# Gate and up projections by seven block products in place of eight, with attention for all tokens moved ahead of the feed-forward part

## The chip, the cores and the metric

The kernel runs on one core of a Trainium2 chip. The metric is device time in microseconds (us). A run that was over 1.5% above the fastest of its kernel counts as slow and is kept out of the ratios.

The engines are named as the profile names them: PE is TensorE (matmuls), PEld its weight loads, DVE is VectorE, ACT is ScalarE, POOL is GpSimd, SP issues the DMAs. In this kernel each engine has its own queue, which keeps the program's order, and waits for the others by semaphores; e1_norm_late below shows what that order alone is worth.

## The reference

A transformer block: pre-norm linear attention with a residual, then a pre-norm gated feed-forward part with a residual. S = 2048 tokens, D = 1024, F = 3584, 32 heads of 32, bf16 inputs.

```python
def _A_ref(x, wqkv, wo):                     # linear attention
    q, k, v = split_heads(x @ wqkv)
    phi = lambda t: where(t > 0, t + 1, exp(t)) + 1e-6
    kv = einsum("bhsd,bhse->bhde", phi(k), v)
    z  = einsum("bhsd->bhd", phi(k))
    o  = einsum("bhqd,bhde->bhqe", phi(q), kv) / (einsum("bhqd,bhd->bhq", phi(q), z)[..., None] + 1e-6)
    return merge_heads(o) @ wo

def _B_ref(x, W_gate, W_up, W_down):         # gated feed-forward
    gate = x @ W_gate
    up   = x @ W_up
    return (gate * (gate > 0) * up) @ W_down

h  = x + _A_ref(layernorm(x), A_wqkv, A_wo)
h2 = h + _B_ref(layernorm(h), B_W_gate, B_W_up, B_W_down)
```

## The kernel before

The kernel is planned in Python: every operation is added to the queue of one engine, and the plan derives the semaphore waits from the buffers that it reads and writes. Each queue keeps the order in which operations were added, so the order of calls is the schedule. Four steps make up the second half of attention:

- `a1(r, ct)`: query projection of one block of 512 tokens and 128 columns (8 matmuls), then the feature map: an exponential on ScalarE and two VectorE steps;
- `a2(st)`: numerators and denominators of a tile of 128 tokens (8 small matmuls), then the division on VectorE;
- `a3`: transpose of the result by DMA;
- `a4(st)`: output projection (16 matmuls), residual, second layer norm.

```python
        def phi(b, w, dst_ap, dst_buf, name):
            ...
            PL.add("act", ... activation(out=Et[:, k, 0:w], in_=src, func=ACTF.Exp) ...)
            PL.add("dve", ... tensor_scalar(E2t, Et, 1.0, 1e-6, op0=ALU.min, op1=ALU.add) ...)
            PL.add("dve", ... scalar_tensor_tensor(dst_ap, src, C1, E2t, op0=ALU.add, op1=ALU.max) ...)

        def a4(r, j, pool):
            ...                                        # 2 x 8 matmuls, residual into hsb
            layernorm(hsb[:, hs, j, :], B_h[hs][j], xn[:, st % NXN, :], B_xn[st % NXN], "dve", "ln2_%d" % st)

        def g_unit(r, ft, pair):                       # one F tile of gate and up, 512 tokens
            for dc in range(NDC):
                mm(bank(ga, SBW), gring[:, sg, dc, fl * P:(fl + 1) * P], hnT[r % 2][:, dc, :], ...)
            for dc in range(NDC):
                mm(bank(gb, SBW), gring[:, su, dc, fl * P:(fl + 1) * P], hnT[r % 2][:, dc, :], ...)
            PL.add("act", ... Relu of bank ga ...)
            PL.add("dve", ... product with bank gb into hhT ...)
```

The feed-forward part handles 512 tokens at a time. The attention steps of the *next* 512 tokens are slipped between its units, so that the numerators and output projections of three of the four token blocks have long runs of gate and up matmuls around them (all query projections come before):

```python
        for r in range(NSB):
            ...
            for ft in range(NFT):
                g_unit(r, ft, pair_of[pidx])
                if bgq:
                    k_, rn, j = bgq.pop(0)
                    run_piece(k_, rn, j, BG)           # one piece of attention of block r + 1
            ...
            for dh in range(ND2):
                d_round(r, dh, ...)                    # down projection
```

## Time and profile before

| | before |
|---|---|
| time, median of 2 | 832.07 us |
| span of the profiled execution | 830.0 us |
| TensorE busy | 99% |
| gate and up matmuls | 1792 |
| spacing of back-to-back 128x512 matmuls | 0.216 us |
| mean granted clock | 1.000 |

The page of the kernel before: busy times, the granted clock in 40 slices (tenths), and the chain of waits followed back from the last instruction.

```profile
PE 823.7 (99%) x4015; PEld 381.3 (46%) x4015; DVE 284.3 (34%) x605; ACT 129.7 (16%) x218; POOL 19.3 (2%) x45
...
PEclk9999999999999999999999999999999999999999
...
PE 98%; DMA 1%; SPq 0%; ACT 0%; DVE 0%; issue 0%; DVEq 0%
```

TensorE is without a wait from 17.6 us on, for 809.4 us, so what counts is the number of matmuls. A busy TensorE is not yet the bound of anything, since records of pipelined matmuls overlap: each lasts 0.38 us in the records, and they start 0.216 us apart. The groups (line, engine, operation, tiles, shapes, count, then busy us and mean ns, then idle time before them) say how many there are. The first two are gate and up, the third is down:

```profile
L474 PE MATMUL ps<-RE,gring 128*128 128x512 bf16 x896 | 196.3, 379 | 0.0
L474 PE MATMUL ps<-RC,gring 128*128 128x512 bf16 x896 | 195.0, 379 | 0.0
L474 PE MATMUL ps<-wdring,RA 128*128 128x512 bf16 x896 | 194.0, 379 | 0.0
```

The timeline of TensorE (start, duration, what) shows attention under cover: numerators (kvz) and output projections (wo) stand between gate and up matmuls (gring), with no idle time in brackets in this stretch:

```profile
203.06 0.63 PE L474 MATMUL ps<-kvz,RB 128*128 128x132 bf16 x8
203.52 3.61 PE L474 MATMUL ps<-RE,gring 128*128 128x512 bf16 x16
...
225.64 3.62 PE L474 MATMUL ps<-wo,RE 128*128 128x512 bf16 x16
229.09 3.62 PE L474 MATMUL ps<-RE,gring 128*128 128x512 bf16 x16
232.55 3.62 PE L474 MATMUL ps<-wo,RE 128*128 128x512 bf16 x16
```

From 229.09 to 232.55 is 3.46 us for 16 matmuls, which is the 0.216 us used throughout.

### The profile page before, as it was taken

The page shows a single profiled execution, that of the slowest core. Times are in us where ns is not written, and L with a number is a line of the kernel's source. Part 1 is how long each engine was busy: PE and PEld are TensorE (multiplying, and loading weights), DVE is VectorE, ACT ScalarE, POOL GpSimd, SP SyncE. Part 2 cuts the span into 40 slices and gives each one's busy share as a digit, 9 for nine tenths or more (in the row PEclk, how much of TensorE's full clock was granted, in tenths as well). Part 3 has the DMA queues.
Part 4 walks back from the last instruction along what each step waited for, and adds up shares of the span by engine and source line. Part 5 has one row for each costly group of instructions (what it writes and reads, how often), then busy time and mean ns, then how long its engine had stood idle before and what let it go on. Part 6 is the DMA issues. An engine that isn't in the chain of part 4 may idle for free.

```text
span 830.0 us, 9935 instructions
## 1 busy us (share of the span) xinstructions
PE 823.7 (99%) x4015; PEld 381.3 (46%) x4015; DVE 284.3 (34%) x605; ACT 129.7 (16%) x218; POOL 19.3 (2%) x45
## 2 busy tenths in 40 slices
PE   8999999999999999999999999999999999999998
PEld 3444444544444444444444444544444444444443
DVE  7455526885552110144511100644111111111111
ACT  4333333312101110001011100111110001111000
POOL 2000000000000000000000000000000000000000
PEclk9999999999999999999999999999999999999999
DMA  9669400230564536545663555555446554443152
GB/s 302 180 188 288 120 13 1 51 78 25 152 177 128 200 104 223 179 131 140 177 187 130 174 182 177 125 173 151 162 150 201 171 159 131 154 151 102 50 167 89
DMA packets 152062, 121.24 MB, mean 146 GB/s; under 512 B 49488, under 2 KB 148048, under 8 KB 152016
## 3 DMA queue, kind: packets, MB, share of 16 engines
q1 hardware_dynamic: 152016, 120.60, 48.3%
q8 instruction: 32, 0.52, 0.3%
q14 instruction: 14, 0.11, 0.0%
HBM read 104.86 MB, written 4.19 MB: 131 GB/s over the span
## 4 chain that ended last, share of the span: by engine, by line
PE 98%; DMA 1%; SPq 0%; ACT 0%; DVE 0%; issue 0%; DVEq 0%
PE ps L474 98%; DMA RB<-in_A_wqkv_dram 1%; SPq L390 0%; PE ps L484 0%; DVE RC L779 0%; ACT Et L533 0%; ACT RA L572 0%; DVEq L112 0%
## 5 line engine op out<-in xcount | busy, mean ns | idle before, releaser
L474 PE MATMUL ps<-RE,gring 128*128 128x512 bf16 x896 | 196.3, 379 | 0.0
L474 PE MATMUL ps<-RC,gring 128*128 128x512 bf16 x896 | 195.0, 379 | 0.0
L474 PE MATMUL ps<-wdring,RA 128*128 128x512 bf16 x896 | 194.0, 379 | 0.0
L754 DVE TENSOR_TENSOR RA<-RC,ps 128x512 bf16<-128x512 bf16 x112 | 76.9, 687 | 249.2 <-PE ps L474 249.2
L752 ACT ACTIVATE RC<-ps 128x512 bf16<-128x512 f32 x112 | 66.9, 597 | 510.3 <-PE ps L474 473.7
L474 PEld LDWEIGHTS ps<-wdring,RA 128*128 128x128 bf16 x896 | 87.7, 98 | 105.7
L474 PEld LDWEIGHTS ps<-RC,gring 128*128 128x128 bf16 x896 | 87.5, 98 | 104.8
L474 PEld LDWEIGHTS ps<-RE,gring 128*128 128x128 bf16 x896 | 87.3, 98 | 103.8
L474 PE MATMUL ps<-RB,RA 128*128 128x512 bf16 x512 | 113.6, 379 | 1.1 <-ACT RA L572 0.7
L779 DVE TENSOR_TENSOR RC<-ps,RF 128x512 bf16<-128x512 f32 x32 | 20.2, 684 | 176.9 <-PE ps L474 176.9
L474 PEld LDWEIGHTS ps<-RB,RA 128*128 128x128 bf16 x512 | 49.1, 98 | 58.3 <-ACT RA L572 0.9
L474 PE MATMUL ps<-wo,RE 128*128 128x512 bf16 x256 | 57.9, 379 | 0.0
L474 PE MATMUL ps<-RA,RC 128*128 128x512 bf16 x256 | 56.7, 379 | 0.0
L533 ACT ACTIVATE Et<-ps 128x512 bf16<-128x512 f32 x64 | 38.2, 597 | 95.5 <-PE ps L474 57.8
L535 DVE TENSOR_SCALAR E2t<-Et 128x512 bf16<-128x512 bf16 x64 | 18.6, 290 | 64.0 <-ACT Et L533 64.0
L474 PEld LDWEIGHTS ps<-wo,RE 128*128 128x128 bf16 x256 | 25.0, 98 | 30.2
L474 PEld LDWEIGHTS ps<-RA,RC 128*128 128x128 bf16 x256 | 24.8, 98 | 29.0
L717 DVE TENSOR_TENSOR RF<-ps,x 128x512 bf16<-128x512 f32 x32 | 22.1, 691 | 24.6 <-PE ps L474 24.5
L512 POOL TENSOR_TENSOR rstd<-ve,neghalf 128x1 f32<-128x1 f32 x32 | 17.5, 548 | 554.5 <-DVE ve L509 554.5
L606 ACT ACTIVATE RE<-ps 128x512 bf16<-128x512 f32 x32 | 19.1, 597 | 36.5 <-PE ps L474 36.5
L538 DVE SCALAR_TENSOR_TENSOR RE<-ps,E2t 128x512 bf16<-128x512 f32 x32 | 22.1, 692 | 1.1
L538 DVE SCALAR_TENSOR_TENSOR RB<-ps,E2t 128x512 bf16<-128x512 f32 x32 | 22.1, 692 | 1.1
(42 smaller groups left out, 168.0 us busy)
## 6 DMA issues: line engine op xcount, KB each, us to landing
gring<-in_B_W_gate_dram SPq DMA_DIRECT2D x28, 1024.0 KB, 5.3
gring<-in_B_W_up_dram SPq DMA_DIRECT2D x28, 1024.0 KB, 7.3
wdring<-in_B_W_down_dram SPq DMA_DIRECT2D x56, 512.0 KB, 3.5
RB<-in_A_wqkv_dram SPq DMA_DIRECT2D x8, 512.0 KB, 8.5
x<-in_A_x_dram SPq DMA_DIRECT2D x16, 256.0 KB, 2.6
out_dram<-RC SPq DMA_DIRECT2D x32, 128.0 KB, 3.8
RE<-in_A_x_dram SPq DMA_DIRECT2D x15, 256.0 KB, 4.7
RC<-in_A_wqkv_dram SPq DMA_DIRECT2D x2, 1024.0 KB, 7.9
```

The costliest lines, as they stand in the source:

```text
L474: lambda e: e.matmul(out_ap, lhsT, rhs, start=start, stop=stop, skip_group_check=skip),
L512: PL.add("pool", lambda e: e.tensor_tensor(out=rstd[:, k, :], in0=ve[:, k, :], in1=neghalf[:], op=ALU.pow), reads=[B_ve[k], B_neghalf], wr ...
L533: PL.add("act", lambda e: e.activation(out=Et[:, k, 0:w], in_=src, func=ACTF.Exp), reads=[B_bank[b]], writes=[B_E[k]], name=name + "_exp")
L535: PL.add("dve", lambda e: e.tensor_scalar(out=E2t[:, k, 0:w], in0=Et[:, k, 0:w], scalar1=1.0, scalar2=1e-6, op0=ALU.min, op1=ALU.add), rea ...
L538: PL.add("dve", lambda e: e.scalar_tensor_tensor(out=dst_ap, in0=src, scalar=C1, in1=E2t[:, k, 0:w], op0=ALU.add, op1=ALU.max), reads=[B_b ...
L606: PL.add("act", lambda e, b=b, j=j: e.activation(out=vv[:, slot, j * GPN:(j + 1) * GPN, 0:P], in_=bank(b, NW).rearrange("p (g w) -> p g w" ...
L717: PL.add("dve", lambda e, b=b, nt=nt: e.tensor_tensor(out=hsb[:, hs, j, nt * NW:(nt + 1) * NW], in0=bank(b, NW), in1=x2[:, xs, nt * NW:(nt ...
L752: PL.add("act", lambda e: e.activation(out=rg[:, k, :], in_=bank(ga, SBW), func=ACTF.Relu), reads=[B_bank[ga]], writes=[B_rg[k]], name="rg ...
L754: PL.add("dve", lambda e: e.tensor_tensor(out=hhT[:, ft, :], in0=rg[:, k, :], in1=bank(gb, SBW), op=ALU.mult), reads=[B_rg[k], B_bank[gb]] ...
L779: PL.add("dve", lambda e, j=j, k=k: e.tensor_tensor(out=outst[:, k, :], in0=bank(banks4[j], NW), in1=hsb[:, hs, j, dh * NW:(dh + 1) * NW], ...
```

## The change

The intent is fewer matmuls. Strassen's scheme multiplies 2x2 blocks with 7 block products in place of 8. Here the blocks are two token blocks of 512, two halves of D and two F tiles of 128, and gate and up each get 7 products of 4 matmuls per pair of F tiles: 56 matmuls, where the plain way takes 64. The price is sums: four sums `S` of activations per pass, four sums `T` of weights for each weight block (fp16, on VectorE), copies of partial results in PSUM (ScalarE), and more elementwise work at the end.

A pass needs both token blocks at once and room for them, so the feed-forward part now runs in two passes of 1024 tokens, and attention for *all* 2048 tokens comes first. The residual and the normalized tokens of the second pass go to scratch space in DRAM and come back. The normalization of the second layer norm moved from VectorE to ScalarE, with a helper step on GpSimd.

The diff, cut to its core:

```diff
+        def a4(st):
+            ...                                             # 16 matmuls into two banks
+            PL.add("dve", ... tensor_tensor(out=hsb[:, hs, :], in0=ps[:, b:b + 2, :], in1=x2, op=ALU.add) ...)
+            ...
+            ks = ln_stats(hsb[:, hs, :], [B_hs[hs]] * NBC, "ln2_%d" % st)
+            PL.add("pool", ... nmr = -mean * rstd ...)
+            PL.add("act", lambda e: e.activation(out=xn[:, kx, :], in_=hsb[:, hs, :], func=ACTF.Identity,
+                                                 bias=nmr[:, ks, :], scale=rstd[:, ks, :]), ...)
+            if st < TPP: dma_t(... hnT ...)                  # first pass: transpose at once
+            else:        dma(... hn_scr ...)                 # second pass: to scratch
...
+            for w in range(2):                               # w: gate, up
+                prod(w, BA[w], w_blk(w, 0, 0), a_blk(0, 0), True, "P1")
+                ident_act(bank(BB[w]), bank(BA[w]), ..., "fk1")
+            for w in range(2):
+                prod(w, BF_[w], t_blk(w, 2), s_blk(2), True, "P7")
+                ident_act(ftmp[:, w, :], bank(BF_[w]), ..., "s7")
+            for w in range(2):
+                prod(w, BB[w], t_blk(w, 1), s_blk(1), False, "P6")
+                ident_act(bank(BC_[w]), bank(BB[w]), ..., "fk2")
+            ...                                              # P2, P5, P4, P3 in the same way
...
+        rest = [(r, ct) for r in range(1, NSB) for ct in range(NG)]
+        LAG = 2
+        for t in range(NST):
+            a2(t)
             if rest:
+                a1(*rest.pop(0))
+            if t >= LAG:
+                a4(t - LAG)
+            if rest:
+                a1(*rest.pop(0))
+            if t == 13:
+                s_sums()
+            if t == 14:
+                for f_ in t_sums(0) + t_sums(1):
+                    f_()
...
+        for p_ in range(NPASS):
+            for q in range(NPAIR):
+                ...
+                strassen_pair(p_, q, fill)
+            for i, (hf, dh) in enumerate(rounds):
+                if p_ + 1 < NPASS and i == 0:
+                    for t in range(TPP):
+                        dma_t(sl_ht[t], hnT[:, :, t * P:(t + 1) * P], hn_scr[t * P:(t + 1) * P, :], ...)
+                d_round(p_, hf, dh, [0, 1, 2, 3] if i % 2 == 0 else [4, 5, 6, 7])
```

## The prediction

> **What bounds it now.** TensorE. The chain of waits is 98% matmuls: one unbroken run of 809.4 us (3936 records) from 17.6 us; granted clock 1.000. Groups: 1792 gate/up and 896 down matmuls; in the timeline 16 of them start 3.455 us apart in total, 0.216 us each. VectorE is busy 34%, ScalarE 16%. The Trainium skill, "TensorE: Matmul & The Clock Gate", section "Back-to-back issue gap", gives N/2.4+2.5 = 216 ns for N=512; the trace agrees.
>
> **What the change removes.** 7 products for 8: gate/up goes from 1792 to 1568 matmuls, 224 x 0.216 = 48.4 us, all on the critical path. Fp16 operands should run at the same rate. Weight traffic for gate/up halves; DMA is not critical.
>
> **What it adds, feed-forward.** A pair of F tiles is 56 matmuls, 12.1 us (28 pairs). Per pair, ScalarE gets 10 evictions (0.6 us each: 6 us) and VectorE 8 operations of about 0.65 us plus 8 weight sums. The skill's "VectorE: DVE Perf Modes", section "The perf-mode tier table", gives tensor_tensor on 16-bit SBUF data 2x, so I estimate (256+150)/0.96 = 0.42 us for a sum (0.69 if 1x): 8.5 to 10.5 us of 12.1. Each copy that a product accumulates upon has two to three products (1.7 to 2.6 us) of slack. So Strassen should remain TensorE-bound. The eight transposes reread between passes (1.24 us issue each) fit before the fifth down-weight chunk is needed (14 us).
>
> **What it moves.** Attention loses its cover. Before, three quarters of it hides under gate/up matmuls; now a tile's iteration holds only numerators (0.46), two query projections (2 x 1.73) and one output projection (3.45): 7.4 us of TensorE. VectorE needs 2.05 (divide) + 2 x 0.92 (feature maps) + about 2.9 (residual and statistics) = 6.8 us, but it doesn't flow: normalization now sits on ScalarE between the two exponentials of an iteration, behind two GpSimd steps. VectorE, in order, waits for the second exponential: statistics end -> rstd (0.80 in the trace) -> negated mean (about 0.4) -> normalization of 1024 (about 1.2) -> exponential (0.6), about 3 us idle. Period about 9.8 us, and TensorE follows through the numerators' single set of banks. Ten such iterations: +24 us. Then:
> - first numerators wait for the last feature map: +2 (another 1 or 2 at token-block boundaries);
> - the last four tiles have no projections left: VectorE-bound (5 against 3.9 us per tile), with the S sums (about 5 us) and first T sums (3.4 us) before the last divisions, and the last output projection waiting for its transpose (about 3.3 us): +15;
> - clock lost after 4 to 6 us gaps: +2.
>
> Lost: about 44 of 48 us. Attention, from the first query projection to the first Strassen product, takes about 160 us instead of 117 us of TensorE work.
>
> **Prediction: 826 us**, 8 in 10 within 805 to 845. Faster by over 2%: 0.24; within 2%: 0.69; slower: 0.07.
>
> **What would show it.** (a) TensorE busy falls to about 775 to 780 us; the Strassen stretches have TensorE idle near 0 and 12.1 us a pair. (b) TensorE idle of some 40 us lies in the attention stretch (about 130 to 290 us), ended by VectorE's division or feature map. (c) VectorE's second feature-map step shows about 3 us wait per tile for the exponential, which waited for the normalization, which waited for GpSimd. (d) Largest single gaps, 4 to 6 us, just before Strassen begins.
>
> **What would make it wrong.** Faster: the GpSimd/ScalarE detour is shorter, or TensorE's lead absorbs it: toward 800. Slower: weight sums at 1x (+6 at the attention's end, less slack per pair), mixed fp16/bf16 matmuls slower, clock throttled in attention's repeated 2 to 3 us gaps, or transposes delaying the first down weights.

## The result, and the profile after

| | before | after |
|---|---|---|
| time, median of 2 | 832.07 us | 852.77 us |
| span of the profiled execution | 830.0 us | 849.7 us |
| TensorE busy | 823.7 us (99%) | 791.0 us (93%) |
| VectorE busy | 284.3 us | 433.2 us |
| mean granted clock | 1.000 | 0.972 |

The ratio of after to before is 1.0248, with a 95% interval of 1.0207 to 1.0288: slower. Ratios here are the mean time of one kernel's fast runs over that of the other's fast runs of the same rounds, so not quite the ratio of the medians. All outputs, here and in every run below, agreed with the reference.

The page after, the same parts:

```profile
PE 791.0 (93%) x3719; PEld 362.6 (43%) x3791; DVE 433.2 (51%) x900; ACT 245.8 (29%) x402; POOL 25.2 (3%) x60
...
PEclk9999999989897899999999989999999999999999
...
PE 81%; DVE 9%; issue 4%; SPq 2%; ACT 1%; POOL 1%; DMA 1%; DVEq 0%; ACTq 0%; POOLq 0%
```

TensorE is no longer alone on the chain, and its clock drops in four of the slices 9 to 14 (170 to 297 us, attention) and in slice 24 (500 us, between the passes). The waits of TensorE (who waited for whom: us in total, times, longest us):

```profile
PE ps L499 <- DVE RAB L538: 24.2, 7, 6.7
...
PE ps L499 <- DVE RO L674: 11.7, 11, 5.6
...
PE ps L499 <- DMA RW<-in_B_W_down_dram: 6.9, 1, 6.9
...
PE ps L499 <- ACT ps L755: 2.8, 1, 2.8
...
PE ps L499 <- DMA RO<-RO: 2.1, 1, 2.1
```

`RAB L538` is the feature map, `RO L674` the division, `RW` a chunk of down weights, `ps L755` a copy of a Strassen partial result, `RO<-RO` the last transpose of attention.

Now one iteration of attention in the timeline, with the chain that paces it (the bracket at the end is the idle time of that engine before it, and what ended it):

```profile
167.63 1.22 DVE L698 TENSOR_TENSOR hsb<-ps,RX 128x1024 bf16<-128x1024 f32 x1
...
170.44 0.15 DVE L514 TENSOR_SCALAR ve<-mv 128x1 f32<-128x1 f32 x1
170.68 0.55 POOL L517 TENSOR_TENSOR rstd<-ve,neghalf 128x1 f32<-128x1 f32 x1 [9.11 <-DVE ve L514]
171.33 0.26 POOL L706 TENSOR_SCALAR nmr<-mv,rstd 128x1 f32<-128x1 f32 x1
171.71 1.24 ACT L710 ACTIVATE xn<-hsb,nmr,rstd 128x1024 bf16<-128x1024 bf16 x1 [7.81 <-POOL nmr L706]
172.85 0.58 ACT L533 ACTIVATE RX<-ps 128x512 bf16<-128x512 f32 x1
173.46 0.29 DVE L535 TENSOR_SCALAR RX<-RX 128x512 bf16<-128x512 bf16 x1 [2.87 <-ACT RX L533]
173.79 0.69 DVE L538 SCALAR_TENSOR_TENSOR RAB<-ps,RX 128x512 bf16<-128x512 f32 x1
...
174.54 0.29 PE L499 MATMUL ps<-kvz,RAB 128*128 128x132 bf16 x1 [6.54 <-DVE RAB L538]
174.62 3.62 PE L499 MATMUL ps<-RAB,RC 128*128 128x512 bf16 x8
178.03 3.74 PE L499 MATMUL ps<-RW,RO 128*128 128x512 bf16 x15
...
182.23 1.23 DVE L698 TENSOR_TENSOR hsb<-ps,RX 128x1024 bf16<-128x1024 f32 x1 [2.25 <-PE ps L499]
```

VectorE ends the statistics (the line `ve`, 170.44 + 0.15) at 170.6 and has nothing to do until 173.46, although the projection whose exponential it waits for was finished long before: ScalarE, in order, first had to do the normalization, which waited for GpSimd. The iteration shown is also one at the end of a token block. There the next numerators need the last feature map, so TensorE, in order, stands still for 6.5 us, and then does the next query projection and output projection, which VectorE in turn waits for. Eight matmuls take about 3.4 us here (174.62 to 178.03), where 1.73 is normal: after the gap TensorE runs at half rate. An iteration inside a block has the same wait of VectorE (2.87 us again, at 188.08 and 198.16).

The residual additions (`hsb`) of tiles 0 to 9 start at 157.54, 167.63, 182.23, 192.33, 202.42, 212.64, 226.63, 236.86, 247.09 and 257.66: a spacing of 10.1 to 10.6, and of about 14 at the two token-block boundaries. The matmuls of an iteration come to 7.37 us.

Between the passes, the queue that issues the DMAs, then TensorE:

```profile
475.75 0.37 SPq L432 DMA_DIRECT2D wring<-in_B_W_up_dram  x1
476.17 12.21 SPq L436 DMA_TRANSPOSE hnT<-hn_scr  x8
488.56 1.87 SPq L432 DMA_DIRECT2D RX<-h_scr  x4
490.53 2.73 SPq L432 DMA_DIRECT2D RW<-in_B_W_down_dram  x4
```

```profile
475.49 13.98 PE L499 MATMUL ps<-RW,RAB 128*128 128x512 bf16 x63
496.39 3.88 PE L499 MATMUL ps<-RW,RAB 128*128 128x512 bf16 x11 [6.93 <-DMA RW<-in_B_W_down_dram]
```

Four chunks of down weights, 14 us of matmuls, are there in advance. The fifth could have been asked for after the first chunk, near 479; it was issued at 490.53, behind eight transposes and four reloads of the residual, and landed 5.8 us later.

And the first Strassen pair (P1 at 301.73, P7 at 303.46, then P6):

```profile
303.46 1.89 PE L499 MATMUL ps<-RC,RE 128*128 128x512 f16 x8
308.12 3.50 PE L499 MATMUL ps<-RC,RE 128*128 128x512 f16 x8 [2.77 <-ACT ps L755]
```

P6 accumulates on a copy that ScalarE makes of P1. That copy stands in ScalarE's queue behind the normalizations of the last tiles.

The account closes. Counts times spacing give 830.0 - 224 x 0.216 = 781.6 us if TensorE had only lost the matmuls. The span is 849.7, so 68.1 us were lost:

| stretch | from, to | takes | its matmuls | lost |
|---|---|---|---|---|
| first query projection to first Strassen product | 128.4, 301.7 | 173.3 | 118.0 | 55.3 |
| first Strassen pair | 301.73, 318.36 | 16.6 | 12.1 | 4.5 |
| first pass's down rounds | 475.49, 580.62 | 105.1 | 96.7 | 8.4 |
| sum (68.1 from the spans; the rest is rounding) | | | | 68.2 |

The other 27 Strassen pairs follow each other at 12.09 us, with no wait.

### The profile page after: what moved, and what is told of

The parts are those of the page before. It is cut to its first block, busy times and chain, and to the rows that moved or that the text cites. A ratio compares the mean times of both kernels' runs of the same rounds, so it can differ in the third digit from the quotient of the medians.

```text
span 849.7 us, 9959 instructions
## 1 busy us (share of the span) xinstructions
PE 791.0 (93%) x3719; PEld 362.6 (43%) x3791; DVE 433.2 (51%) x900; ACT 245.8 (29%) x402; POOL 25.2 (3%) x60
## 4 chain that ended last, share of the span: by engine, by line
PE 81%; DVE 9%; issue 4%; SPq 2%; ACT 1%; POOL 1%; DMA 1%; DVEq 0%; ACTq 0%; POOLq 0%
PE ps L499 81%; DVE st L509 2%; DVE hsb L698 2%; DVE RO L674 1%; SPq L436 1%; ACT RX L533 1%; DVE RAB L538 1%; DVE RX L535 1%; DMA RW<-in_B_W_down_dram 1%; POOL rstd L517 1%; DVE rden L667 0%; DVE RC L728 0%; DVE dtmp L663 0%; DVE mv L512 0%; DMA RO<-RO 0%
## 5 line engine op out<-in xcount | busy, mean ns | idle before, releaser
L499 PE MATMUL ps<-RW,RAB 128*128 128x512 bf16 x878 | 194.3, 381 | 7.9 <-DMA RW<-in_B_W_down_dram 6.9
L499 PE MATMUL ps<-RC,RE 128*128 128x512 f16 x672 | 156.0, 382 | 2.8 <-ACT ps L755 2.8
L499 PEld LDWEIGHTS ps<-RW,RAB 128*128 128x128 bf16 x896 | 87.9, 98 | 113.9 <-DMA RW<-in_B_W_down_dram 7.4
L499 PE MATMUL ps<-RAB 128*128 128x512 bf16 x499 | 112.4, 379 | 1.6 <-ACT RAB L571 0.7
L755 ACT ACTIVATE ps<-ps 128x512 f32<-128x512 f32 x112 | 65.1, 582 | 161.2 <-PE ps L499 160.6
L499 PE MATMUL ps<-hnT,wring 128*128 128x512 bf16 x448 | 105.8, 379 | 0.0
L499 PEld LDWEIGHTS ps<-RC,RE 128*128 128x128 f16 x672 | 66.0, 98 | 83.3 <-ACT ps L755 3.3
L755 ACT ACTIVATE RO<-ps 128x512 f32<-128x512 f32 x112 | 66.7, 597 | 53.9 <-PE ps L499 53.9
L499 PE MATMUL ps<-RW,RO 128*128 128x512 bf16 x249 | 62.4, 403 | 2.7 <-DMA RO<-RO 2.1
L499 PE MATMUL ps<-RAB,RC 128*128 128x512 bf16 x250 | 64.2, 407 | 0.4
L710 ACT ACTIVATE xn<-hsb,nmr,rstd 128x1024 bf16<-128x1024 bf16 x16 | 19.8, 1240 | 114.1 <-POOL nmr L706 114.1
L755 ACT ACTIVATE RAB<-ps 128x512 bf16<-128x512 f32 x56 | 33.4, 597 | 62.0 <-PE ps L499 62.0
L499 PE MATMUL ps<-kvz,RAB 128*128 128x132 bf16 x128 | 14.2, 230 | 36.6 <-DVE RAB L538 24.2
```

Source lines behind the costliest of these rows:

```text
L499: lambda e: e.matmul(out_ap, lhsT, rhs, start=start, stop=stop, skip_group_check=skip),
L710: PL.add("act", lambda e: e.activation(out=xn[:, kx, :], in_=hsb[:, hs, :], func=ACTF.Identity, bias=nmr[:, ks, :], scale=rstd[:, ks, :]), ...
L755: PL.add("act", lambda e: e.activation(out=dst, in_=src, func=func), reads=reads, writes=writes, name=name)
```

## The experiments

Theory A says that queue order did this: the normalization stands between two exponentials, and VectorE, TensorE and the DMA queue each wait in order for something that they need not wait for. Rival B says that VectorE is simply too full once attention has lost its cover (6.8 us of work per 7.4 us). Rival C puts it on the clock.

Times are compared with the changed kernel's 852.77, which was not run again beside them; ratios are against before, run on the same chip. The kernel before took 832.07 us in the changed kernel's rounds and 831.5 and 831.8 in those of the experiments, so the two comparisons differ by under 0.1%.

### e1_norm_late: the normalization after the second projection

```diff
-            ks = ln_stats(...)                      # then nmr, norm2 and its DMA, all in a4
+            ln2_k[st] = ln_stats(...)
+        def a4n(st):                                # nmr, norm2 and its DMA
             ...
                 a4(t - LAG)
             if rest:
                 a1(*rest.pop(0))
+            if t >= LAG:
+                a4n(t - LAG)
```

> The changed kernel with one reorder: the negated mean, the normalization on ScalarE and the transfer behind it are issued after the second query projection of an iteration, not between the two. Nothing else changes, no work is added or removed. Theory A (in-order queues: VectorE waits about 3 us per tile because the second exponential stands behind the normalization on ScalarE): the spacing of the residual additions falls from 10.15 us to 7.4-7.8, at token-block boundaries from 14.2 to about 10; total 815 to 828 us. Rival B (VectorE is simply too full in attention, 6.8 of 7.4 us, so where the normalization stands is irrelevant): within 6 us of the changed kernel's 852. Rival C (the lowered clock is the cause, waits are the effect of nothing in the order): within 6 us too.

Measured: 819.02 us, ratio 0.985 (0.9825 to 0.9876). No operation was added or taken away, and the kernel got 33.7 us faster. The residual additions are now 7.4 us apart inside a block (182.03, 189.28, 196.66) and 9.8 to 11.2 at boundaries. ScalarE does the exponential before the normalization, and VectorE no longer idles:

```profile
183.64 0.60 ACT L533 ACTIVATE RX<-ps 128x512 bf16<-128x512 f32 x1 [2.93 <-PE ps L499]
...
184.85 0.15 DVE L514 TENSOR_SCALAR ve<-mv 128x1 f32<-128x1 f32 x1
184.92 0.28 DVE L535 TENSOR_SCALAR RX<-RX 128x512 bf16<-128x512 bf16 x1
```

VectorE's busy time hardly changed (432.7 against 433.2 us), so rival B falls for this part. The clock rose to 0.987 without anything done to it: it followed the waits, which goes against C as the first cause. (e3 says more on C: it has the old pace at the full clock.)

### e2_norm_twice: the normalization done twice

```diff
-            PL.add("act", ... norm2 ...)
+            for _ in range(2):
+                PL.add("act", ... norm2 ...)
```

> The changed kernel with the normalization on ScalarE done twice (same values written again; the result stays right), which costs ScalarE 16 x 1.15 us while it is idle 71% of the time. Theory A: the normalization lies on the loop that paces attention, so each of about 10 iterations grows by 1.1 us: +8 to +14 us. Rival B (VectorE throughput): 0 to +3 us.

Measured: 868.54 us, 15.8 above the changed kernel, ratio 1.0446. The direction and place are those of A, the size is above the range that I gave. The spacing inside a block grew from about 10.1 to 11.35, and at boundaries from 14.3 to 15.9; from the first to the tenth residual addition that is 12.1 us more. What I had left out is that the doubled step also stands before the first Strassen pair's copies, where TensorE's wait grew from 2.8 to 4.0 us, and before the last tiles. The wait for the down weights, which the edit does not touch, was 8.0 us here against 6.9. An engine that idles 71% of the time passes an extra 1.2 us per tile on in full: 12.1 us over nine intervals are 1.3 each.

### e3_lead_two: two query projections ahead

```diff
         LAG = 2
         fill = []
+        for _ in range(2):
+            a1(*rest.pop(0))
```

> The changed kernel with two query projections of the next token block moved before the first numerators, so that each token block's feature maps are complete one iteration before they are needed. Theory A (at a boundary TensorE, in order, waits for the last feature map and only then starts the projection that VectorE needs next, 4 us per boundary, partly at half clock): three boundaries of 14.2 become 10.15 and the first 1.4 us wait goes: 836 to 842 us. Rival (a boundary only shifts the wait, VectorE's total is what counts): within 4 us of 852.

Measured: 836.12 us, ratio 1.0062 (1.0045 to 1.0079), 16.6 below the changed kernel. The additions are 10.1 to 10.2 us apart up to the ninth (the tenth follows after 9.3), so the boundaries are gone and the pace of the loop is what it was. The clock is 1.00 from 170 to 220 us, the number before the DMA share in this line of stretches (busy us of PE, PEld, DVE, ACT and POOL come first):

```profile
170.00:220.00 50.00, 39.45 (x194) 16.83 (x197) 33.34 (x75) 11.04 (x15) 4.06 (x10) 1.00 0.41 106
```

So rival C falls for the pace inside a block: at the full clock it is still 10.1 us. TensorE waits 1.9 to 2.0 us in each iteration there, and the low clock of the boundaries went with their gaps of 6.5 us. That does not explain all of it: the changed kernel also ran at half rate for some 3 us after waits of 1.6 and 1.8 us inside blocks (from 201.8 and 246.7 on), which similar waits here did not bring. The kernel before also had two query projections issued ahead; the change had dropped them, and e3 puts them back.

### e4_spread: the transposes spread over two down rounds

```diff
-                if p_ + 1 < NPASS and i == 0:
-                    for t in range(TPP):
-                        dma_t(...)                                   # all eight
-                d_round(p_, hf, dh, ...)
+                fl = []
+                if p_ + 1 < NPASS and i < 2:
+                    for t in range(i * TPP // 2, (i + 1) * TPP // 2):
+                        fl.append(lambda t=t: dma_t(...))            # one after each chunk
+                d_round(p_, hf, dh, ..., fill=fl)
```

> The changed kernel with the eight transposes between the passes issued one after each chunk of the first two down rounds, not all before the first. Theory (the 12.2 us of issue on the one queue delay the fifth down-weight chunk, TensorE waits 6.9 us and then runs a while at half clock): the wait goes, 843 to 846 us. Rival (the transposes slow the loads by taking the DMA engines, wherever they stand): the wait is spread, 849 us or more.

Measured: 842.47 us, ratio 1.0133 (1.0117 to 1.0148), 10.3 below the changed kernel and half a microsecond better than the range. In the profiled runs the span fell by 8.3 us, from 849.7 to 841.4. The first pass's down rounds take 96.7 us (475.65 to 572.35), which is their matmuls and nothing else. The fifth chunk is now asked for at 479.35, and TensorE has no gap:

```profile
479.35 0.38 SPq L432 DMA_DIRECT2D RW<-in_B_W_down_dram  x1
479.77 1.55 SPq L436 DMA_TRANSPOSE hnT<-hn_scr  x1
...
475.65 34.70 PE L499 MATMUL ps<-RW,RAB 128*128 128x512 bf16 x157
```

The same loads and transposes go through the same queue, and TensorE does not wait, so it was the order of issue, not the load on the DMA engines.

### e5_plain and e5b_plain: the restructuring without Strassen

```diff
-            ... P1, P7, P6, P2, P5, P4, P3 with their copies ...
+            for n_, (t, h) in enumerate(((0, 0), (0, 1), (1, 0), (1, 1))):
+                for w in range(2):
+                    prod(w, bb[w], w_blk(w, 0, h), a_blk(0, t), True, "M0")
+                    prod(w, bb[w], w_blk(w, 1, h), a_blk(1, t), False, "M1")
+                ident_act(r11[:, n_ % 2, :], bank(bb[0]), ..., "rl", func=ACTF.Relu)
+                PL.add("dve", ... hh = bank(bb[1]) * r11 ...)
-            ... all S and T sums ...
```

> The changed kernel with its order, passes and buffers, but each pair of F tiles computed by the plain 8 block products (64 matmuls) and no S or T sums: the restructuring alone. If Strassen by itself is worth what the count says, this is slower than the changed kernel by 224 x 0.216 = 48.4 us, less about 8 us of sums at the attention's end and up to 4 us of the first pair's wait that plain products do not have: 884 to 896 us, so the restructuring alone costs 52 to 64 us against before. Rival: Strassen's copies and sums cost time in the feed-forward stage itself; then this gains on it there, and the total is under 875.

Measured: 889.73 us (median of four; the three fast ones lie between 888.67 and 889.78), ratio 1.0694 (1.0677 to 1.071). So the new order by itself costs 58 us against before, inside the range, and the rival (under 875) falls. Against the changed kernel it is 37 us slower and not 48.4: there Strassen lost again some 12 us to its own sums before the last divisions (7.6, see below) and to the first pair (4.5). One of its four runs, the one that was profiled, took 1079.26 us at a mean clock of 0.772. It is a slow run, I have no cause for it, and nothing here rests on it. To see the stages, the same kernel was run once more.

> The same kernel as e5_plain again, for a profile in the fast state (the profiled execution of e5_plain had a mean clock of 0.772 and took 1077 us). Feed-forward stretches should show no TensorE waits: a pair takes 64 x 0.216 = 13.8 us against 12.1 with Strassen; the attention's spacing is that of the changed kernel, 10.1 and 14.2 us.

Measured: 888.46 us (one run, so its state is unknown, but it agrees with the fast runs of e5_plain). Its attention has the spacing of the changed kernel (157.82, 167.90, 182.25, ...), and the same 24.2 us of TensorE waits for the feature map. The first product comes at 294.08, 7.6 us earlier than with Strassen, because VectorE has no sums to make before the last divisions.

### e6_three: the three edits together

The edits of e1, e3 and e4.

> The changed kernel with the three edits together: normalization after the second projection, two projections ahead, transposes spread. e1 took 33.7 us, e3 16.6, e4 10.3; e1 and e3 overlap at the token-block boundaries, where e1 still waits some 9 us. Additive otherwise: 796 to 803 us. Left are about 12 us at the end of attention and 4 us in the first pair. If the three are parts of one thing (VectorE's total), the sum stops short: over 808.

Measured: 802.08 us, ratio 0.9641 (0.9627 to 0.9654). Singly the edits took 33.7, 16.6 and 10.3 us, 60.6 in sum; together they took 50.7. That is the range expected, since e1 and e3 both act on the token-block boundaries. TensorE's largest waits are then those at the end of attention and in the first pair:

```profile
245.46 1.45 PE L499 MATMUL ps<-kvz,RAB 128*128 128x132 bf16 x8 [5.56 <-DVE RO L674]
257.64 3.61 PE L499 MATMUL ps<-RW,RO 128*128 128x512 bf16 x15 [2.35 <-DMA RO<-RO]
267.48 3.25 PE L499 MATMUL ps<-RC,RE 128*128 128x512 f16 x8 [2.77 <-ACT ps L760]
```

### e7_five: the first weight sums early, the last normalizations late

```diff
+        t01 = t_sums(0) + t_sums(1)
         for ct in range(NG):
             a1(0, ct)
+            if 3 <= ct <= 6:
+                t01.pop(0)()
+                t01.pop(0)()
...
-            if t == 14:
-                for f_ in t_sums(0) + t_sums(1): f_()
-            a4n(t)                                  # for the last three tiles
+                strassen_pair(p_, q, fill)
+                if p_ == 0 and q < 3:
+                    a4n(13 + q)
```

> e6_three with two more edits: the first eight T sums of weights on VectorE during the first eight query projections, where it is half idle, and the normalizations of the last three tiles (needed in the second pass only) issued after the first, second and third Strassen pair, so that they do not stand before that pair's copies on ScalarE. Expected: 3 us less at the end of attention and 3 to 4.5 us less in the first pair: 789 to 796 us. If the first pair's wait had another cause, over 795.

Measured: 795.4 us, ratio 0.9566 (0.9553 to 0.9579), 6.7 below e6. The total does not decide whether the first pair's wait had the suspected cause (the two ranges, 789 to 796 and over 795, overlap), but the trace does: the wait for ScalarE is gone from the list of waits. Of the two edits made together only the late normalizations touch ScalarE's queue, so they were its cause.

### e8_pool_sums: the first S sums on GpSimd

```diff
-            if t == 13:
-                s_sums()
+            if 10 <= t <= 13:
+                s_sums("pool")[t - 10]()            # one sum per iteration
```

> e7_five with the first four S sums on GpSimd, one per iteration from the eleventh on, not on VectorE after the fourteenth tile. VectorE loses 4.9 us in the stretch where it is the bound: 3 to 5 us less than e7_five. If GpSimd needs over 6 us for a sum of 2048, or the two slow each other, no gain or a loss.

Measured: 790.05 us, ratio 0.9499 (0.9486 to 0.9512), 5.4 below e7, slightly more than expected. A sum takes 4.06 us on GpSimd and 1.22 on VectorE, but GpSimd had the time. TensorE is the chain again, at the full clock. The page's busy times and chain, and what is left of TensorE's waits:

```profile
PE 774.7 (98%) x3719; PEld 359.8 (46%) x3791; DVE 427.5 (54%) x896; ACT 246.9 (31%) x402; POOL 40.5 (5%) x64
...
PE 93%; DVE 4%; issue 1%; ACT 1%; DMA 0%; POOL 0%; SPq 0%; DVEq 0%; ACTq 0%; POOLq 0%
```

```profile
PE ps L499 <- DVE RO L674: 2.6, 7, 0.6
...
PE ps L499 <- DMA RO<-RO: 1.5, 1, 1.5
```

The waits for the feature map, for the down weights and for ScalarE's copies are no longer in the list. Attention takes 125.0 us (128.4 to 253.4) for 118.0 us of matmuls.

### e9_plain_repaired: the repaired order without Strassen

The order of e8 with the plain products of e5, and no sums.

> Attention first with the repairs (normalization late, two projections ahead, transposes spread, last normalizations deferred), but the plain 8 products and no sums. Against e8_pool_sums it lacks only Strassen. If Strassen is worth its 224 matmuls and nothing else: 790 + 48 = 838 us, less up to 2 us of sums that e8 still carries: 835 to 840 us. Then the repaired order alone costs 3 to 8 us against before, and nearly all of the net gain is Strassen's. If Strassen's copies cost anything on TensorE's path: under 832.

Measured: 838.55 us, ratio 1.0085 (1.0071 to 1.0098). Against e8 the difference is 48.5 us, and 224 matmuls at 0.216 us are 48.4. (The two ran on different chips, where the kernel before took 831.5 and 831.8 us.) Strassen pays exactly what it removes, and its sums and copies cost TensorE nothing once they stand in the right place. The repaired order costs 7 us against before.

## Why the prediction was wrong

The prediction was 826 us, within 805 to 845, most likely within 2% of before. Measured were 852.77, slower by 2.5%. The loss of cover and the wait behind the normalization were foreseen, and rightly. The steps that failed are four terms of the sum: the token-block boundaries ("another 1 or 2"), the clock ("+2"), the transposes that "fit", and the slack of the copies in the first pair. Point by point:

1. **What bounded the kernel before, and the gain of 48.4 us.** Right. e9 against e8 shows 48.5. (The formula cited there is the page's for one isolated matmul; see the first point of the last section.)
2. **The feed-forward stretch stays bound by TensorE at 12.1 us a pair.** Right for 27 of 28 pairs (12.09 us), with VectorE's sums at the estimated rate (0.42 us a `T` sum). This agrees with the Trainium skill, "VectorE: DVE Perf Modes", section "The perf-mode tier table", which puts `tensor_tensor` on bf16 data in SBUF at twice the base rate; the trace shows 0.42 us also where bf16 goes in and fp16 comes out. Fp16 and mixed products run at the spacing of bf16: 56 of them in 12.09 us are 0.216 us each.
3. **The loop of attention: "Period about 9.8 us ... Ten such iterations: +24 us".** Right in mechanism and size; VectorE's wait for the exponential, "about 3 us" in the prediction, is 2.87. Inside a token block the spacing is about 10.1; e1 takes the cause away and it falls to 7.4, e2 doubles the suspected step and it rises to 11.35. Over the nine intervals, 10.1 against 7.37 makes 25 us.
4. **Token-block boundaries: "another 1 or 2".** This was the first step that failed: the term was mis-sized. Each of the two boundaries inside the loop took about 4.2 us more than an ordinary interval (14.60 and 13.99 against 10.1), and a third follows after the tenth addition (13.6). I had delayed the numerators by the feature map, but had forgotten that TensorE, in order, holds the next query projection and output projection behind them, which VectorE then waits for: 5.2 us of matmuls, or about 7 where half of the clock is gone. e3, which moves two projections ahead and does nothing else, ends this and gained 16.6 us.
5. **End of attention: "+15" and "clock lost ... +2".** From the tenth addition to the first product 44.1 us passed, and the matmuls that stand behind that tile's output projection come to 24.3 us (some 2 us of them had run before the addition): 19.8 lost. In e3, where the third boundary is gone, the same stretch (250.02 to 285.77) takes 35.8 us for 22.6 us of matmuls, 13.2 lost. So the end alone cost less than the 17 predicted, and the third boundary brought it above. The clock term failed. The prediction expected TensorE idle for "some 40 us" in attention and busy for 775 to 780 us in all. Idle it was for 39.7 us there (173.30 less 133.61 in the first line below, which has the form of the one under e3), but busy for 791.0 in all. The same matmuls kept it busy for 119.67 us in e8 (second line) and for about 14 us more here, at a mean clock of 0.89:

```profile
128.40:301.70 173.30, 133.61 (x630) 60.05 (x641) 118.37 (x271) 34.54 (x46) 13.17 (x29) 0.89 0.34 86
...
128.40:253.40 125.00, 119.67 (x632) 57.24 (x644) 112.83 (x267) 34.34 (x45) 27.84 (x32) 1.00 0.47 121
```

   That the idle time came out as predicted is partly luck, since slow matmuls filled some of the waits. e7 and e8 together got about 12 us out of this stretch and the first pair.
6. **"The eight transposes reread between passes ... fit before the fifth down-weight chunk is needed."** Wrong, and this was another step that failed: 8.4 us. The prediction set 8 x 1.24 = 9.9 us of issue against 14 us of matmuls. In the queue the transposes stand behind two weight loads that wait for the last products of the last pair, so they began at 476.2, after the pass's last product; they took 12.2 us; four reloads of the residual, 1.9 us, came after; and the chunk, issued at 490.53, needed 5.8 us to land, while TensorE was through with the other four at 489.5. The size of the issue was not the point: with 9.9 us in place of 12.2 the chunk would still have landed near 494 (an estimate: 476.2 + 9.9 + 2.0 + 5.8). What was left out is all that follows the transposes, above all the landing. e4 removed the wait.
7. **The first Strassen pair: "Each copy ... has two to three products ... of slack".** This failed at the start: 4.5 us, 2.8 of wait and 1.6 of matmuls at half rate after it. The slack was reckoned against the products around the copy, for a pair in the middle, where ScalarE's queue holds nothing but that pair's copies. At the start the queue still held normalizations. e7 removed the wait.

In one sum: the prediction had about 44.5 us of losses, and the trace has 68.1. Of the difference of about 24 us, 8.4 are the transposes, 4.5 the first pair, about 8.3 the two boundaries inside the loop (33.8 lost from the first to the tenth addition, against 24 and 1 or 2 predicted) and 2.8 the end of attention. Part of these terms is the half rate of the matmuls after the gaps. Where others then waited for TensorE, the trace allows an estimate: against 0.216 us each, the matmuls right after the three boundary waits took 1.8, 1.4 and 2.8 us too long (from 174.62, 219.77 and 264.79 on), after the first pair's wait 1.6 and after the wait for down weights 1.4, 9 us in all where the prediction had 2. No run separated half rate from order; but the clock did not act on its own, since it went to 1.000 in e8 as the gaps went, with no edit aimed at it.

The verdict in the other direction was within reach of the same reading: the change was slower for the order of a few calls. With them moved it beats both kernels (e7, 795.4 us), and with the first `S` sums also given to GpSimd it takes 790.05 us, 5% below before.

## What to carry to other kernels

Here removing matmuls paid in full only once what they had hidden was put in order, so before taking a cover away, follow one iteration around all the in-order queues, not only engine by engine. In each queue ask what stands in front of the operation that somebody waits for: a long step behind a slow helper (here a normalization behind two GpSimd steps) belongs after the short step that feeds the critical engine, and a DMA that is needed soon does not belong behind eight that are not. Check the seams separately, meaning first and last iterations, block boundaries and the change of passes, since a check made in mid-loop says nothing about them.

## What the Trainium skill lacked or had wrong

- "TensorE: Matmul & The Clock Gate", section "Back-to-back issue gap", says that in a stream of weight loads and matmuls the sustained spacing at N=512 is about 131 ns and that the N/2.4 + 2.5 formula over-counts there. Here thousands of such pairs run at 0.216 us, which is the formula's 216 ns. The prediction used the formula, and was right to, but did not say that the page sets it aside for streams.
- The same page, section "Why this matters for your kernels", advises against TensorE gaps over about 3 us. Mostly the runs agree: after gaps of 5.5 to 6.7 us matmuls were 0.43 us apart for some microseconds, and the repeated gaps of about 1.9 us in e3 left the clock at 1.00 (170 to 220 us). But in e1 one gap of 2.0 us (ending at 200.7) was followed by about 3 us at half rate, while two gaps alike (1.9 and 2.2 us) were not; in the changed kernel waits of 1.6 and 1.8 us were. A short gap is not always safe; what decides was not tested.
- "GPSIMD Engine Reference", section "When to use GPSIMD", table "Engine selection", puts VectorE about 2x ahead for two-input elementwise work and names no data type in that row. With 16-bit SBUF data it was 3.3x: 4.06 us against 1.22 for 2048 elements per partition. Off the critical path it still gained 5.4 us.
- No page gives, for this chip, the time in which one queue issues DMA transposes of 128x1024. Here one took 1.24 us from SBUF and 1.31 us from DRAM (medians); the eight between the passes took 12.2 us to issue, and the loads behind them waited.
